# Linear attention and a gated feed-forward block: how the first batch's q is cast and turned, and the order of its first steps

## The chip, the cores and the metric

The kernel runs on one core of a Trainium2 chip. A core has a matrix engine (TensorE; PE in the profile, and PEld for its weight loads), a vector engine (VectorE, DVE), a scalar engine (ScalarE, ACT), GpSimd (POOL) and a sync engine (SP). Each engine works through its own instructions in order, and they wait for each other by semaphores. Here POOL and SP only issue DMAs, apart from a few small steps. The metric is the device time of one execution in microseconds. The kernel before takes 314.32 us in the median of five runs (313.93 to 314.49).

## The reference

Eight batches of eight heads, 576 tokens, 64 columns, go through linear attention, and the result through a gated feed-forward block over all 4608 tokens:

```python
phi = lambda x: np.where(x > 0, x, np.exp(x) - 1.0) + 1.0
q_p, k_p = phi(q), phi(k)
kv  = np.einsum('bhsd,bhse->bhde', k_p, v)
z   = np.sum(k_p, axis=2)
num = np.einsum('bhsd,bhde->bhse', q_p, kv)
den = np.einsum('bhsd,bhd->bhs', q_p, z)[..., None] + 1e-06
x   = (num / den).transpose(0, 2, 1, 3).reshape(B * S, H * D)
g   = x @ w_gate                       # 512 -> 1536
out = (g / (1 + np.exp(-g)) * (x @ w_val)) @ w_out   # 1536 -> 512
```

phi(x) is max(x, 0) + min(exp(x), 1), and the kernel computes it in that form, or, where x + 1 is at hand, as min(max(x + 1, 1), exp(x)).

## The kernel before

Everything is computed in fp16 with fp32 sums. The tokens of a batch are cut into 64 groups of nine neighbours: a partition holds one group (64 partitions for each half of the heads, 128 together), and j = 0..8 is the token in the group. Heads come in two parts, lp = 0 and 1, of two heads each per half. The feed-forward block works on nine groups g of 512 tokens (8 values of j of 64 tokens each). For each, layer 1 (`l1`, L292, with `l1_post`) takes 12 blocks fb of 128 columns, a gate and a value product in each, four steps of contraction c; layer 2 (`l2_mm`, L299) brings the 1536 columns back to 512. While group g is in these layers, the attention of the next batches is done between the products by the other engines. The order of all work is written out by hand: the order of the lines is the order on each engine, and nothing reorders it.

Loads are issued by POOL, mostly fp32 in memory to fp16 on the core, in a fixed order (L335 to L353): k and v of batch 0, the first weights, and so on; eight semaphores are used in turn, so a load waits for the one eight places ahead of it. Only q of batch 0 comes as fp32 by two SP DMAs, into `q32`, heads 0 and 1 first.

The change touches the time before the first full layer 1 block, in which batch 0 is prepared (L456 to L516), and the last token group of batch 0's q later on (`exp_q8`, `phi_q8`, called in `period0`). In the order of the program:

- Casts (L460 to L463): q32 to fp16 in `qr[0]`, head by head, three on DVE, the one of head 1 on ACT.
- `q_one` puts 1.0 into two pairs of PSUM banks; `q_turn` adds the transpose of q to it, by products with the identity `id16`: one product for each of two heads and each of eight j, 64 output rows each. So q + 1 stands there, turned.
- `q_exp(lp, h)` (ACT, L450 through L120) takes exp(q + 1 - 1) from half h of a pair to `qT`; `q_phi(lp, h)` (DVE, L454) joins it with the pair to phi(q).
- `exp_k`, `mx_k`, `mn_k`, `add_k` make phi of k: ek = exp on ACT, kp = max(k, 0), ek = min(ek, 1), kp = kp + ek on DVE.
- `zt` (L411) sums phi(k) over tokens by products, from kp before and from ek after the min, so that the sum needs no add; `zr_copy` spreads it to `Zr`. `kv_corner` (L185) makes k.v, 36 products of 64x64 for one operand and part; for lp = 0 it uses the added kp, for lp = 1 the kp and the ek one after the other. `r_copy` copies it to `R`.
- `t_corners` (L254) multiplies turned q with `Zr` (the denominators) and with `R` (the numerators); `lnrd` takes 1/x as exp(-ln x), four ACT steps for one lp; `x_t` (L424) multiplies the two into `xT`.
- `l1_mm` (L276) are the first two blocks of layer 1, taken step by step of c as chunks of `xT` get ready: c = 0 and 1 need `x_t(0,0)`, c = 2 and 3 the two halves of `x_t(0,1)`.
- `warm(n)` are n products without use of 128x512 (L124). `WARM` holds the six counts, in the order of the calls.

Of the kernel before, what the change touches and what calls it, by code (L numbers as in the profile page):

```python
# [9 lines left out]
AF = mybir.ActivationFunctionType  # L10
ALU = mybir.AluOpType
AX = mybir.AxisListType

P = 128
# [3 lines left out]
def kernel(  # L18
# [10 lines left out]
    nc = tc.nc  # L29

    B, H, S, D = q.shape
# [4 lines left out]
    J = S // C  # L36
# [3 lines left out]
    EPS = 1e-6  # L40
    SC = 4096.0
    NB = 3
    WARM = (4, 1, 4, 4, 2, 2)

    sb = ctx.enter_context(tc.tile_pool(name="sb", bufs=1))
    pp = ctx.enter_context(tc.tile_pool(name="ps", bufs=1, space=bass.MemoryType.PSUM))
# [2 lines left out]
    def many(shape, dt, name, n=2):  # L49
        return [sb.tile(shape, dt, name=f"{name}_{i}") for i in range(n)]  # L50

    kr = many([P, HL, J * D], FP16, "kr", NB)
    qr = many([P, HL, J * D], FP16, "qr", NB)
    vr = many([P, HL, J * D], FP16, "vr", NB)
    ek = many([P, 2, J, 2 * D], FP16, "ek")
    eq = many([P, HL, J * D], FP16, "eq")
    kp = many([P, 2, J, 2 * D], FP16, "kp")
    qp = many([P, 2, J, 2 * D], FP16, "qp")
# [6 lines left out]
    q32 = sb.tile([P, HL, J * D], FP32, name="q32")  # L65
# [16 lines left out]
    id16 = sb.tile([P, P], FP16, name="id16")  # L82
# [36 lines left out]
    def act(out, in_, func=AF.Copy, scale=1.0, bias=0.0):  # L119
        nc.scalar.activation(out=out, in_=in_, func=func, bias=bias, scale=scale)  # L120

    def warm(n, w=512, ps=None):
        for _ in range(n):
            nc.tensor.matmul(out=(ps or pp4[1][1])[:, 512 - w:512], lhsT=ones[:, :],  # L124
                             rhs=ones[:, 0:1].to_broadcast([P, w]), start=True, stop=True)
# [4 lines left out]
    def jl(t, b, lp):  # L130
        return t[b % 2][:, lp, :, :].rearrange("p j (l d) -> p l j d", d=D)

    def lj(t, b, lp):
        return t[b % NB][:, hs(lp), :].rearrange("p l (j d) -> p l j d", d=D)

    def exp_k(b, lp):
        act(jl(ek, b, lp), lj(kr, b, lp), AF.Exp)
# [4 lines left out]
    def mx_k(b, lp):  # L142
        nc.vector.tensor_scalar(out=jl(kp, b, lp), in0=lj(kr, b, lp), scalar1=0.0, scalar2=None, op0=ALU.max)  # L143

    def mn_k(b, lp):
        a = ek[b % 2][:, lp, :, :]
        nc.vector.tensor_scalar(out=a, in0=a, scalar1=1.0, scalar2=None, op0=ALU.min)  # L147
# [9 lines left out]
    def add_k(b, lp):  # L157
        a = kp[b % 2][:, lp, :, :]
        nc.vector.tensor_tensor(out=a, in0=ek[b % 2][:, lp, :, :], in1=a, op=ALU.add)  # L159
# [19 lines left out]
    def kv_corner(b, lp, t, first, last):  # L179
        ps = kvp[b]  # L180
        for j in range(J):
            for l2 in range(2):
                for hh in range(2):
                    rows = slice(C * hh, C * hh + C)
                    nc.tensor.matmul(out=ps[hh][D * l2:D * l2 + D, D * lp:D * lp + D],  # L185
                                     lhsT=t[b % 2][rows, lp, j, D * l2:D * l2 + D],
                                     rhs=vr[b % NB][rows, 2 * lp + l2, D * j:D * j + D],
                                     start=(first and j == 0), stop=(last and j == J - 1))
# [6 lines left out]
    def r_copy(b, l0, l1, engs):  # L195
        for hh in range(2):
            src = kvp[b][hh][:, D * l0:D * l1].rearrange("p (l d) -> p l d", d=D)
            if engs[hh] == "A":
                act(R[b % 3][:, l0:l1, hh, :], src)
            else:  # L200
                nc.vector.tensor_copy(out=R[b % 3][:, l0:l1, hh, :], in_=src)
# [38 lines left out]
    def units(g):  # L240
        us = [(u // J, u % J) for u in range(U * g, U * g + U)]
        res = []
        for b in sorted(set(u[0] for u in us)):
            js = [j for (bb, j) in us if bb == b]
            res.append((b, js[0], js[-1] + 1, C * us.index((b, js[0]))))
        return us, res
# [3 lines left out]
    def corners(ps, W, b, lp, j0, j1, c0):  # L250
        for l2 in range(2):
            rows = slice(D * l2, D * l2 + D)
            for hh in range(2):
                nc.tensor.matmul(out=ps[l2][C * hh:C * hh + C, c0:c0 + C * (j1 - j0)],  # L254
                                 lhsT=W[rows, lp, hh, :], rhs=qt(b, lp, hh, j0, j1)[rows],
                                 start=True, stop=True)
# [75 lines left out]
    for h in (0, 2):  # L332
        nc.sync.dma_start(out=q32[:, h:h + 2, :],
                          in_=q[0].rearrange("(l a) (c j) d -> (a c) l (j d)", a=2, j=J)[:, h:h + 2, :])
# [59 lines left out]
    def copy8(b, ps):  # L394
        nc.vector.tensor_copy(out=qT[b][:, :, 8, :, :].rearrange("p l h c -> p l (h c)"),
                              in_=ps[:, 256 * b:256 * b + P].bitcast(FP16).rearrange("p (l c) -> p l c", l=2))

    def exp_q8():
        act(eq[0][:, :, D * 8:D * 9], qr[0][:, :, D * 8:D * 9], AF.Exp)

    def phi_q8():
        r, e = qr[0][:, :, D * 8:D * 9], eq[0][:, :, D * 8:D * 9]
        nc.vector.tensor_scalar(out=r, in0=r, scalar1=0.0, scalar2=None, op0=ALU.max)
        nc.vector.tensor_scalar(out=e, in0=e, scalar1=1.0, scalar2=None, op0=ALU.min)
        nc.vector.tensor_tensor(out=qp[0][:, :, 8, :].rearrange("p a (l d) -> p a l d", d=D),
                                in0=e.rearrange("p (a l) d -> p a l d", l=2),
                                in1=r.rearrange("p (a l) d -> p a l d", l=2), op=ALU.add)

    def zt(b, lp, ps, t, first, last):
        for j in range(J):  # L410
            nc.tensor.matmul(out=ps[:, 0:2], lhsT=t[b % 2][:, lp, j, :], rhs=ob[:, 0:P:C],  # L411
                             start=(first and j == 0), stop=(last and j == J - 1))

    def zr_copy(b, lp, ps):
        nc.vector.tensor_scalar(out=Zr[b][:, lp, :, :], in0=ps[:, 0:2].unsqueeze(2).to_broadcast([P, 2, D]),
                                scalar1=1.0 / SC, scalar2=None, op0=ALU.mult)
# [9 lines left out]
    def x_t(g, lp, ps, l2s=(0, 1)):  # L426
        for l2 in l2s:
            xmul(xT[g % 2][:, 2 * lp + l2, :], ps[l2][:, :], rd[lp][:, l2, :])

    def t_corners(g, W, lp, ps):  # L430
        for (b, j0, j1, c0) in units(g)[1]:
            corners(ps, W[b], b, lp, j0, j1, c0)

    def q_one(pair_):
        for h in range(2):
            nc.tensor.matmul(out=pair_[h][:, :], lhsT=part[:, :], rhs=ones[:, 0:1].to_broadcast([P, 512]),
                             start=True, stop=False)

    def q_turn(lp, pair_):
        for l2 in range(2):  # L440
            for j in range(J - 1):
                nc.tensor.matmul(out=pair_[j // 4][D * l2:D * l2 + D, P * (j % 4):P * (j % 4) + P],  # L442
                                 lhsT=qr[0][:, 2 * lp + l2, D * j:D * j + D], rhs=id16[:, :],
                                 start=False, stop=(j % 4 == 3))

    def q_half(lp, h):
        return qT[0][:, lp, 4 * h:4 * h + 4, :, :].rearrange("p j h c -> p (j h c)")

    def q_exp(lp, h, pair_):
        act(q_half(lp, h), pair_[h][:, :], AF.Exp, bias=m1[:, 0:1])  # L450

    def q_phi(lp, h, pair_):
        a = q_half(lp, h)
        nc.vector.scalar_tensor_tensor(out=a, in0=pair_[h][:, :], scalar=1.0, in1=a, op0=ALU.max, op1=ALU.min)  # L454
# [2 lines left out]
    X = [pp4[0][0], pp4[3][0]]  # L457
    Y = [pp4[3][1], pp4[0][1]]
    qa, qb = pp4[2], pp4[0]
    nc.vector.tensor_copy(out=qr[0][:, 0, :], in_=q32[:, 0, :])  # L460
    act(qr[0][:, 1, :], q32[:, 1, :])
    nc.vector.tensor_copy(out=qr[0][:, 2, :], in_=q32[:, 2, :])
    nc.vector.tensor_copy(out=qr[0][:, 3, :], in_=q32[:, 3, :])  # L463
    warm(WARM[0])
    q_one(qa)
    q_one(qb)
    q_turn(0, qa)
    q_exp(0, 0, qa)
    q_exp(0, 1, qa)
    warm(WARM[1])  # L470
    q_turn(1, qb)
    q_exp(1, 0, qb)
    exp_k(0, 0)
    q_exp(1, 1, qb)
    warm(WARM[2])
    exp_k(0, 1)
    q_phi(0, 0, qa)
    q_phi(0, 1, qa)
    mx_k(0, 0)
    q_phi(1, 0, qb)  # L480
    mn_k(0, 0)
    mx_k(0, 1)
    zt(0, 0, X[1], kp, True, False)
    warm(WARM[3])
    zt(0, 0, X[1], ek, False, True)
    zr_copy(0, 0, X[1])
    warm(WARM[4])
    t_corners(0, Zr, 0, pp4[2])
    lnrd(pp4[2], 0)
    add_k(0, 0)  # L490
    q_phi(1, 1, qb)
    zt(0, 1, Y[0], kp, True, False)
    kv_corner(0, 0, kp, True, True)
    r_copy(0, 0, 1, "VV")
    warm(WARM[5], ps=X[0])
    mn_k(0, 1)
    t_corners(0, R, 0, X)
    zt(0, 1, Y[0], ek, False, True)
    zr_copy(0, 1, Y[0])
    x_t(0, 0, X, (0,))  # L500
    kv_corner(0, 1, kp, True, False)
    t_corners(0, Zr, 1, Y)
    lnrd(Y, 1)
    x_t(0, 0, X, (1,))
    kv_corner(0, 1, ek, False, True)
    r_copy(0, 1, 2, "VV")
    l1_mm(0, 0, pp4[2], (0,))
    l1_mm(0, 1, X, (0,))
    t_corners(0, R, 1, pp4[1])
# [264 lines left out]
```

## Time and profile before

| what | us |
|---|---|
| median of five runs | 314.32 |
| the profiled execution | 314.49 |
| its span | 312.7 |
| TensorE busy | 306.1 (98%) |
| DVE busy | 204.8 (66%) |
| ACT busy | 152.7 (49%) |
| first product of the first full layer 1 block (L292) starts at | 19.04 |

The span is the time from the first to the last instruction; 1.8 us lie around it. Busy shares are of the whole span. What happens in the first 20 us is not seen in them, but in the chain of what was waited for, read in the order of time, and in the order of instructions on each engine.

### The profile page before, as it was taken

How to read it: one execution, taken by the hardware profiler on the slowest of the kernel's cores; microseconds unless marked ns; L12 is line 12 of the kernel's file. 1: busy time of each engine (PE TensorE's matmuls, PEld its weight loads, DVE VectorE, ACT ScalarE, POOL GpSimd, SP SyncE). 2: the span in 40 equal slices, each digit the busy share in tenths (PEclk: the TensorE clock that was granted, in tenths of full speed). 3: DMA queues.
4: the chain of work that ended last, by engine and by line, in shares of the span. 5: the costliest groups of instructions: out<-in, count | busy, mean ns of one | idle time of the engine just before them, and what ended most of it. 6: DMA issues, size and time to landing. Idle time of an engine off the chain costs nothing.

```text
span 312.7 us, 5593 instructions
## 1 busy us (share of the span) xinstructions
PE 306.1 (98%) x2221; PEld 142.8 (46%) x2221; DVE 204.8 (66%) x361; ACT 152.7 (49%) x231; POOL 48.8 (16%) x73
## 2 busy tenths in 40 slices
PE   8989999999999999999999999999999999999994
PEld 4534444444544454445444544454444444444442
DVE  4854868999699667977697859874981434143410
ACT  4955959539633845375535643475330333133311
POOL 8745434400000410032001400000000000000000
PEclk9999999999999999999999999999999999999999
DMA  8999999998512594229612990514032300140014
GB/s 216 197 197 199 206 207 235 235 207 124 116 32 39 82 190 129 40 43 183 176 29 49 142 222 2 75 43 93 0 70 60 82 1 3 41 94 2 0 34 101
DMA packets 41178, 32.80 MB, mean 105 GB/s; under 512 B 16448, under 2 KB 36160, under 8 KB 41152
## 3 DMA queue, kind: packets, MB, share of 16 engines
q0 software_dynamic: 20480, 18.29, 37.4%
q1 hardware_dynamic: 20592, 14.13, 19.3%
q8 instruction: 17, 0.28, 0.3%
q14 instruction: 9, 0.07, 0.1%
q10 hardware_dynamic: 80, 0.03, 0.0%
HBM read 37.75 MB, written 9.44 MB: 151 GB/s over the span
## 4 chain that ended last, share of the span: by engine, by line
PE 96%; DMA 1%; DVE 1%; issue 0%; ACT 0%
PE pp L292 57%; PE pp L299 30%; PE pp L276 2%; PE pp L254 2%; PE pp L185 2%; DMA q<-in_q_dram 1%; PE pp L124 1%; DVE qT L454 0%; PE pp L411 0%; PE pp L442 0%; ACT qT L120 0%; PE pp L212 0%; PE pp L374 0%; DVE osb L322 0%; DVE kp L143 0%
## 5 line engine op out<-in xcount | busy, mean ns | idle before, releaser
L120 ACT ACTIVATE sil<-pp 128x512 f16<-128x512 f32 x108 | 63.4, 597 | 102.0 <-PE pp L292 101.0
L292 PE MATMUL pp<-xT,wg 128*128 128x512 f16 x416 | 106.8, 379 | 0.0
L292 PE MATMUL pp<-xT,wv 128*128 128x512 f16 x416 | 106.8, 379 | 0.0
L285 DVE SCALAR_TENSOR_TENSOR hT<-pp,sil 128x512 f16<-128x512 f32 x108 | 72.3, 681 | 49.3 <-PE pp L292 35.8
L299 PE MATMUL pp<-wo,hT 128*128 128x512 f16 (+2 forms) x444 | 97.1, 373 | 0.6 <-DVE osb L322 0.6
L299 PEld LDWEIGHTS <-hT 128*128 128x128 f16 x444 | 41.9, 98 | 49.9 <-issue 2.1
L292 PEld LDWEIGHTS <-wv 128*128 128x128 f16 x416 | 40.7, 98 | 49.1
L292 PEld LDWEIGHTS <-wg 128*128 128x128 f16 x416 | 40.7, 98 | 48.4
L322 DVE TENSOR_SCALAR osb<-pp 128x512 f32<-128x512 f32 (+1 forms) x19 | 12.9, 682 | 31.1 <-PE pp L299 31.1
L120 ACT ACTIVATE osb<-pp 128x512 f32<-128x512 f32 (+1 forms) x18 | 10.3, 574 | 34.8 <-PE pp L299 34.8
L120 ACT ACTIVATE ek<-kr 128x1152 f16<-128x1152 f16 x16 | 17.9, 1157 | 0.1
L120 ACT ACT_TABLE_LOAD x13 | 16.7, 1283 | 2.5 <-PE pp L292 2.4
L705 POOL COPY gate<-qT 128x1 f16<-128x1 f16 x4 | 1.3, 315 | 96.4 <-DMA qT<-qp 96.4
L229 DVE TENSOR_TENSOR qp<-qp,rden 128x1152 f16<-128x1152 f16 x12 | 16.2, 1347 | 0.0
L220 DVE TENSOR_REDUCE den<-prod 128x18 f32<-128x1152 f16 x12 | 16.1, 1343 | 0.0
L120 ACT ACTIVATE eq<-qr 128x1152 f16<-128x1152 f16 (+1 forms) x15 | 15.9, 1104 | 0.0
L271 DVE TENSOR_SCALAR xT<-pp 128x512 f16<-128x512 f32 (+1 forms) x14 | 8.8, 667 | 6.6 <-PE pp L254 6.6
L103 POOL DMA_DIRECT2D vr<-in_v_dram x16 | 11.8, 740 | 8.3 <-DMA kr<-in_k_dram 3.5
L103 POOL DMA_DIRECT2D kr<-in_k_dram x16 | 11.5, 722 | 9.3 <-DMA vr<-in_v_dram 3.0
L159 DVE TENSOR_TENSOR kp<-ek,kp 128x1152 f16<-128x1152 f16 x15 | 11.4, 758 | 0.5
L103 POOL DMA_DIRECT2D qr<-in_q_dram x14 | 10.1, 725 | 4.9 <-DMA qr<-in_q_dram 1.1
L147 DVE TENSOR_SCALAR ek<-ek 128x1152 f16<-128x1152 f16 x16 | 7.8, 486 | 4.5 <-ACT ek L120 4.5
(85 smaller groups left out, 180.9 us busy)
## 6 DMA issues: line engine op xcount, KB each, us to landing
out_dram<-osb SPq DMA_DIRECT2D x70, 128.0 KB, 2.8
kr<-in_k_dram POOLq DMA_DIRECT2D x16, 288.0 KB, 8.6
vr<-in_v_dram POOLq DMA_DIRECT2D x16, 288.0 KB, 9.4
qr<-in_q_dram POOLq DMA_DIRECT2D x14, 288.0 KB, 11.4
wg<-in_moe_w_gate_dram POOLq DMA_DIRECT2D x5, 256.0 KB, 9.7
wv<-in_moe_w_val_dram POOLq DMA_DIRECT2D x5, 256.0 KB, 10.1
q<-in_q_dram SPq DMA_DIRECT2D x2, 576.0 KB, 4.2
wo<-in_moe_w_out_dram POOLq DMA_DIRECT2D x2, 512.0 KB, 12.5
```

Of the source, the lines that this page charges most:

```text
L103: nc.gpsimd.dma_start(out=dst[b % NB][:, 2 * lp:2 * lp + 2, :], in_=src[b].rearrange("(l a) (c j) d -> (a c) l (j d)", a=2, j=J)[:, 2 * lp ...
L120: nc.scalar.activation(out=out, in_=in_, func=func, bias=bias, scale=scale)
L147: nc.vector.tensor_scalar(out=a, in0=a, scalar1=1.0, scalar2=None, op0=ALU.min)
L159: nc.vector.tensor_tensor(out=a, in0=ek[b % 2][:, lp, :, :], in1=a, op=ALU.add)
L185: nc.tensor.matmul(out=ps[hh][D * l2:D * l2 + D, D * lp:D * lp + D], lhsT=t[b % 2][rows, lp, j, D * l2:D * l2 + D], rhs=vr[b % NB][rows, 2 ...
L220: nc.vector.tensor_reduce(out=den[:, c, :], in_=prod[:, :, :].rearrange("p j (l d) -> p (j l) d", d=D), axis=AX.X, op=ALU.add)
L229: nc.vector.tensor_tensor(out=qv, in0=qv, in1=rden[:, c, :].unsqueeze(2).to_broadcast([P, 2 * J, D]), op=ALU.mult)
L271: nc.vector.tensor_scalar(out=dst, in0=ps[l2][:, c0:], scalar1=1.0 / SC, scalar2=None, op0=ALU.mult)
L285: nc.vector.scalar_tensor_tensor(out=hT[g % 2][:, fb, :], in0=ps[1][:, :], scalar=SC, in1=s[:, :], op0=ALU.mult, op1=ALU.mult)
L292: nc.tensor.matmul(out=ps[h][:, :], lhsT=w[:, c, P * fb:P * fb + P], rhs=xT[g % 2][:, c, :], start=(c == 0), stop=(c == 3))
L299: nc.tensor.matmul(out=l2p[(g, t)][:, n0:n1], lhsT=hT[g % 2][:, fb, P * t:P * t + P], rhs=wo[:, fb, n0:n1], start=(fb == 0), stop=(fb == F ...
L322: nc.vector.tensor_scalar(out=o[:, n0:n1], in0=ps[:, n0:n1], scalar1=1.0 / SC, scalar2=None, op0=ALU.mult)
```

## The change

q of batch 0 is cast into `qp[0]` in place of `qr[0]`: for each j the two heads of a part stand beside each other, 128 columns, and only j = 0 to 7 are cast. `q_turn` then takes one product with 128 rows for each j in place of two with 64. The ninth token, which is not turned here, is taken from `q32` by `exp_q8` and `phi_q8`. In the order of steps: `q_exp(1,1)` comes ahead of `exp_k(0,0)`; `q_phi(1,0)` ahead of `mx_k(0,0)`, and `q_phi(1,1)` right behind it; `mn_k(0,1)` follows `add_k(0,0)`; the second half of `zt(0,1)` with its `zr_copy` comes ahead of the numerators of lp = 0; both terms of `kv_corner(0,1)` and its `r_copy` come ahead of `t_corners(0, Zr, 1)`. The counts of warm products are (4, 2, 5, 4, 2, 1) in place of (4, 1, 4, 4, 2, 2).

```diff
-    WARM = (4, 1, 4, 4, 2, 2)
+    WARM = (4, 2, 5, 4, 2, 1)
...
+    def q8(t):
+        return t[:, :, D * 8:D * 9].rearrange("p (a l) d -> p a l d", l=2)
     def exp_q8():
-        act(eq[0][:, :, D * 8:D * 9], qr[0][:, :, D * 8:D * 9], AF.Exp)
+        act(q8(eq[0]), q8(q32), AF.Exp)
     def phi_q8():
-        r, e = qr[0][:, :, D * 8:D * 9], eq[0][:, :, D * 8:D * 9]
-        nc.vector.tensor_scalar(out=r, in0=r, scalar1=0.0, scalar2=None, op0=ALU.max)
-        nc.vector.tensor_scalar(out=e, in0=e, scalar1=1.0, scalar2=None, op0=ALU.min)
...
+        r = qp[0][:, :, 8, :].rearrange("p a (l d) -> p a l d", d=D)
+        nc.vector.tensor_scalar(out=r, in0=q8(q32), scalar1=0.0, scalar2=None, op0=ALU.max)
+        nc.vector.tensor_scalar(out=q8(eq[0]), in0=q8(eq[0]), scalar1=1.0, scalar2=None, op0=ALU.min)
+        nc.vector.tensor_tensor(out=r, in0=q8(eq[0]), in1=r, op=ALU.add)
...
     def q_turn(lp, pair_):
-        for l2 in range(2):
-            for j in range(J - 1):
-                nc.tensor.matmul(out=pair_[j // 4][D * l2:D * l2 + D, P * (j % 4):P * (j % 4) + P],
-                                 lhsT=qr[0][:, 2 * lp + l2, D * j:D * j + D], rhs=id16[:, :],
-                                 start=False, stop=(j % 4 == 3))
+        for j in range(J - 1):
+            nc.tensor.matmul(out=pair_[j // 4][:, P * (j % 4):P * (j % 4) + P],
+                             lhsT=qp[0][:, lp, j, :], rhs=id16[:, :],
+                             start=False, stop=(j % 4 == 3))
...
-    nc.vector.tensor_copy(out=qr[0][:, 0, :], in_=q32[:, 0, :])
-    act(qr[0][:, 1, :], q32[:, 1, :])
...
+    def q_cast(h):
+        return dict(out=qp[0][:, h // 2, 0:8, D * (h % 2):D * (h % 2) + D],
+                    in_=q32[:, h, 0:8 * D].rearrange("p (j d) -> p j d", d=D))
+    nc.vector.tensor_copy(**q_cast(0))
+    act(**q_cast(1))
...
     q_exp(1, 0, qb)
+    q_exp(1, 1, qb)
     exp_k(0, 0)
-    q_exp(1, 1, qb)
     warm(WARM[2])
     exp_k(0, 1)
     q_phi(0, 0, qa)
     q_phi(0, 1, qa)
+    q_phi(1, 0, qb)
     mx_k(0, 0)
-    q_phi(1, 0, qb)
+    q_phi(1, 1, qb)
     mn_k(0, 0)
...
     add_k(0, 0)
-    q_phi(1, 1, qb)
+    mn_k(0, 1)
     zt(0, 1, Y[0], kp, True, False)
     kv_corner(0, 0, kp, True, True)
     r_copy(0, 0, 1, "VV")
+    zt(0, 1, Y[0], ek, False, True)
     warm(WARM[5], ps=X[0])
-    mn_k(0, 1)
+    zr_copy(0, 1, Y[0])
     t_corners(0, R, 0, X)
-    zt(0, 1, Y[0], ek, False, True)
-    zr_copy(0, 1, Y[0])
     x_t(0, 0, X, (0,))
     kv_corner(0, 1, kp, True, False)
+    kv_corner(0, 1, ek, False, True)
+    r_copy(0, 1, 2, "VV")
     t_corners(0, Zr, 1, Y)
     lnrd(Y, 1)
     x_t(0, 0, X, (1,))
-    kv_corner(0, 1, ek, False, True)
-    r_copy(0, 1, 2, "VV")
```

More of the change, by code (lines that the diff above doesn't have):

```diff
@@ L396, in copy8 @@
                               in_=ps[:, 256 * b:256 * b + P].bitcast(FP16).rearrange("p (l c) -> p l c", l=2))
+    def q8(t):
+        return t[:, :, D * 8:D * 9].rearrange("p (a l) d -> p a l d", l=2)
     def exp_q8():
-        act(eq[0][:, :, D * 8:D * 9], qr[0][:, :, D * 8:D * 9], AF.Exp)
+        act(q8(eq[0]), q8(q32), AF.Exp)
     def phi_q8():
-        r, e = qr[0][:, :, D * 8:D * 9], eq[0][:, :, D * 8:D * 9]
-        nc.vector.tensor_scalar(out=r, in0=r, scalar1=0.0, scalar2=None, op0=ALU.max)
-        nc.vector.tensor_scalar(out=e, in0=e, scalar1=1.0, scalar2=None, op0=ALU.min)
-        nc.vector.tensor_tensor(out=qp[0][:, :, 8, :].rearrange("p a (l d) -> p a l d", d=D),
-                                in0=e.rearrange("p (a l) d -> p a l d", l=2),
-                                in1=r.rearrange("p (a l) d -> p a l d", l=2), op=ALU.add)
+        r = qp[0][:, :, 8, :].rearrange("p a (l d) -> p a l d", d=D)
+        nc.vector.tensor_scalar(out=r, in0=q8(q32), scalar1=0.0, scalar2=None, op0=ALU.max)
+        nc.vector.tensor_scalar(out=q8(eq[0]), in0=q8(eq[0]), scalar1=1.0, scalar2=None, op0=ALU.min)
+        nc.vector.tensor_tensor(out=r, in0=q8(eq[0]), in1=r, op=ALU.add)
     def zt(b, lp, ps, t, first, last):
@@ L459 @@
     qa, qb = pp4[2], pp4[0]
-    nc.vector.tensor_copy(out=qr[0][:, 0, :], in_=q32[:, 0, :])
-    act(qr[0][:, 1, :], q32[:, 1, :])
-    nc.vector.tensor_copy(out=qr[0][:, 2, :], in_=q32[:, 2, :])
-    nc.vector.tensor_copy(out=qr[0][:, 3, :], in_=q32[:, 3, :])
+    def q_cast(h):
[3 more added lines that the diff above has]
+    act(**q_cast(1))
+    nc.vector.tensor_copy(**q_cast(2))
+    nc.vector.tensor_copy(**q_cast(3))
     warm(WARM[0])
```

## The prediction

> **What bounds the kernel now.** I read the page's engine row and its chain first, then the chain in order of time for the first 22 us, then the order of instructions on TensorE, VectorE (DVE) and ScalarE (ACT) there, and last the DMA queues in windows of one microsecond.
>
> The page: first the engine row, then the clock row (tenths of full speed per slice), the row of instruction loads, and the chain's shares.
>
> ```profile
> PE 306.1 (98%) x2221; PEld 142.8 (46%) x2221; DVE 204.8 (66%) x361; ACT 152.7 (49%) x231; POOL 48.8 (16%) x73
> ...
> PEclk9999999999999999999999999999999999999999
> ...
> q8 instruction: 17, 0.28, 0.3%
> ...
> PE 96%; DMA 1%; DVE 1%; issue 0%; ACT 0%
> ```
>
> TensorE is the bound, and from 19.04 us on (first product of L292) it has almost no gap: a microsecond won or lost in the prologue arrives whole at the end, if TensorE afterwards finds everything in place. The change works in the prologue, so its chain decides (start, length, what):
>
> ```profile
> 0.74 3.77 DMA q<-in_q_dram
> ...
> 6.18 0.70 ACT qT L120
> 6.88 0.02 issue
> 6.90 1.29 DVE qT L454 x2
> 8.19 0.48 DVE kp L143
> 8.67 0.05 issue
> 8.72 0.39 PE pp L411 x9
> ...
> 13.37 0.39 PE pp L254 x4
> 13.76 0.34 PE pp L185 x36
> ...
> 16.86 0.89 issue
> 17.75 1.45 PE pp L276 x6
> ```
>
> Two things are to be seen. Up to 8.72 the chain goes through the first half of q (the two q_phi of L454), then `mx_k(0,0)` (L143), then the first z. And at 16.86 TensorE stands for 0.89 us on "issue": no semaphore holds it, in the middle of `l1_mm` (third product of c = 2; its operands were there for the first two).
>
> I take that stop for a late load of TensorE's own instructions. The DMA view of 15 to 16 us has this row, none in the windows before it:
>
> ```profile
> q0 software_dynamic: 380, 0.19, 138.8%
> q8 instruction: 1, 0.02, 5.9%
> ```
>
> Evidence: 17 loads of 0.28 MB are 16 KB each; 4442 TensorE instructions (products and weight loads) over 17 are about 256 each. When the DMA is idle (88, 125, 237, 262, 289 us), load k starts just as instruction 256k - 104 begins. Number 152 begins at 10.98 us, but q0 is full and the packet starts only at 15.26; it takes 0.95 and TensorE goes on at 17.75, at instruction 450. So from the request to going on it is 6.4 to 6.8 us, and the block is missed 298 instructions after the request's mark.
>
> Here a rule is to be weighed. The Trainium skill ("Runtime: NRT & Kernel Launch", section "Instruction fetch mechanics") says that blocks of 256 instructions are fetched while the current one executes, and that crossing a boundary costs one tail bump, mostly hidden. By the rule the stop is nothing of this kind, stays where it is in the program, and the change has only the longer chain worked out below (+0.62). The row says 0.89 us, with the queue of 16 KB loads starting 1.6 us before it. I follow the row.
>
> **The change, part by part.**
>
> *Instruction count.* `q_turn` goes from 32 products to 16 (8 per call instead of 16): -16. The warm products go from 17 to 18: +1. Each has a weight load: 30 instructions fewer before the stop's place. The 450th instruction, now in c = 2, is then old number 480. c = 3 ends at old 460, so the new place is ten products into L292. With TensorE reaching L292 at 18.65 (below), that is 18.65 + 9 x 0.216 = 20.6. The request: the mark falls into `kv_corner(0,0)`, at about 11.9 to 12.2 (old 11.0 to 11.3 plus 0.9). Plus the measured 6.4 to 6.8: 18.3 to 19.0. The block is there 1.6 us or more before it is needed, and the stop costs nothing; its cover is the products of c = 1 to 3 and the first ten of L292. Later loads: number 3 is asked at 41.8 instead of 40.8 and missed at 48.7 instead of 47.5; about the same 6.9 us. Without the stop, before's c = 3 would have waited for its input alone: `x_t(0,1)` ends at 16.42 + 0.69 = 17.11, c = 3 at 17.17, not 18.18. **Stop gone: -1.01.**
>
> *First turn and casts.* ACT's cast of head 1 has 512 instead of 576 columns: by the slope between 128x1152 (1153 ns) and 128x576 (683 ns), 0.63 us, done at 5.16. Eight products, still at half clock (107 ns apart in the trace at 5.05 to 6.23), start at 5.22, the fourth ends at 5.86, so `q_exp(0,0)` starts at 5.92 (6.18 before). The 0.26 is worth nothing on its own: DVE must first cast heads 2 and 3, which the DMA releases at 5.97. Those casts write runs of 64 at a stride of 128. No fp32 cast does so in the trace; the nearest row is L384, which writes the same strided form at 452 ns for 128x1152, as fast as the contiguous L147 (460). So I take the present rate: 33 ns less each, head 3 done at 6.79 (6.85 before). Bounds: 0.43 us each, or 0.69 if the strided write halves the rate (+0.5 on the path).
>
> *Second turn.* Products from 6.84, 56 ns apart; the fourth ends at 7.25; `q_exp(1,0)` 7.31 to 8.00 (7.42 before).
>
> *Order on DVE and ACT.* `q_phi(1,0)` now stands ahead of `mx_k(0,0)`. It waits for `q_exp(1,0)`: starts at 8.03. `mx_k(0,0)` follows 0.60 later (start to start, as at 7.51 and 8.10 before): 8.63, ends at 9.19, and behind it waits the first z on TensorE: 9.24 instead of 8.72, **+0.52**. `exp_k(0,0)` is behind `q_exp(1,1)`: 8.5 to 9.66 (9.16 before); `mn_k(0,0)` 9.74 to 10.20. The four warm products after the first z end at 10.39, so `mn_k` is hidden by 0.14 us; without it the z.ek part would wait for it. z.ek 10.39 (9.84): +0.54; `zr_copy` 10.80, `t_corners(Zr,0)` 11.15 and `lnrd(0)` on ACT 11.59 (11.05). `exp_k(0,1)` ends at 10.72 (10.79), nobody waits.
>
> `q_phi(1,1)` left its place behind `add_k(0,0)`; `mn_k(0,1)` stands there now, ending at 12.12 (12.52 before): z.ek of lp = 1 runs right after `kv_corner(0,0)`, `zr_copy(0,1)` ends 0.35 earlier. This hangs on no end: the next reader waits longer for something else.
>
> *Both k.v terms ahead of `t_corners(Zr,1)`.* `t_corners(R,0)` starts at 12.76 (12.21, +0.55), then kv kp and kv ek, 0.43 each with the step between (12.90 to 13.35 before): 13.96 for `t_corners(Zr,1)`, against 13.35. One z.ek of 0.37 less ahead of it, one kv more: **+0.62 in all**. Behind it waits `lnrd(1)`, four ACT steps of 2.59 together (13.80 to 16.39), now 14.41 to 17.01. `r_copy(0,1)` is 0.3 to 0.4 earlier, but `t_corners(R,1)` stays behind c = 0 at about 15.3 to 15.4 (15.00), so that gain has no taker. `x_t(0,1)` second half: 17.04 to 17.73. c = 3 starts at 17.78, L292 at 18.65. What is late next would be weights: `fb` = 2 lands at 17.32 (gate) and 18.09 (value), needed 18.65 and 19.5; covered. Layer 2 parts land 1.2 us or more ahead.
>
> *Last token group (period 0).* `exp_q8` and `phi_q8` read q32: one max on 128x256 in fp32 instead of fp16, 0.23 to about 0.36 us (estimate from the cast's rate). DVE then idles 0.36 us for `exp_k(1,0)`; hidden. No DMA is added or moved; POOL's load into `qr[0]` at 50 us loses a wait that was long met, and SP has nothing new.
>
> **Sum.** +0.62 - 1.01 = -0.39 us. The profiled execution took 314.49 (span 312.7 and 1.8 around it): 314.1. It is the slowest of the five shown; against the median of 314.32 it is 313.93, and I predict **313.9**.
>
> **Rivals.**
> 1. *The new order costs only about 0.2.* The 0.52 rests on DVE durations in a crowded stretch: `mx_k(0,0)` took 556 ns, the same form later 450; q's second half may land sooner; kv's pair may take 0.34 each. Together up to 0.4 less: 313.5. Against it: the wait of `q_phi(1,0)` on the second turn is in the order itself.
> 2. *The stop does not go* (the load comes later, or it was no load and sits at this place in the program). Then +0.62 stays: 314.9. For it: how long q0 holds the packet back (4 us here) is one sample of a full queue; other loads under traffic waited 3 to 4 us, none the 6 needed.
> 3. *The clock falls back* (the slower side). TensorE would idle 0.8 us from the last of the five warm products (8.42) to the first z (9.24), then do little dense work. The skill's "TensorE: Matmul & The Clock Gate", section "Part 1: The HAM clock gate", gives a busy window of about 3.4 us and half clock after an idle one. If it decided against the window up to about 9.65, warm and corner products until 13.06 double: four warm (0.75), corners (0.3), kv (0.4): +1.5, 315.4. [...]against it, the 0.89 us stop left the clock at 1.00.
> 4. *The casts lose their double rate*: +0.5, 314.4.
>
> **How the numbers follow.** A measurement of this kernel tells about 0.2% (0.63 us) from no change: faster is under 313.69, slower over 314.95. Main case 0.55, with its own range 313.4 to 314.4, since the stop's size and the chain each are good to some 0.3; about 4 in 10 of it are faster (0.22), the rest the same (0.33). Rival 1: 0.19, all faster. Rival 2: 0.16, on the border, 0.11 slower and 0.05 same. Rival 3: 0.05, slower. Rival 4: 0.05, 0.04 same and 0.01 slower. Sums: faster 0.41, same 0.42, slower 0.17. The range is 313.3 (rival 1's side) to 315.0 (rival 2 held).
>
> **What would show it.** Right: no "issue" piece near 17 us; the first z at about 9.2, `mx_k(0,0)` after three q_phi; `t_corners(Zr,1)` near 14.0; L292 from 18.5 to 18.8; a 16 KB load at about 16. Wrong: an "issue" piece some ten products into L292 (rival 2), products of 512 columns 0.43 apart after 9 us (rival 3), casts of 0.6 or more (rival 4), first z before 9.0 (rival 1).

## The result, and the profile after

The changed kernel takes 313.54 us (median), the one before 314.14 us in the same comparison. The ratio is 0.9981, with a 95% interval of 0.9976 to 0.9987: it is 0.6 us faster (0.4 to 0.75), a small gain, but clear of no change. The profiled execution took 313.39 us with a span of 311.6 (before: 314.49 and 312.7). The two profiles lie 1.1 us apart and the medians only 0.6, since before's profiled execution was 0.35 us slower than its median and the changed kernel's 0.15 faster.

The page after, engine row, clock row and instruction loads:

```profile
PE 304.8 (98%) x2206; PEld 141.6 (45%) x2206; DVE 204.9 (66%) x361; ACT 152.6 (49%) x231; POOL 48.3 (16%) x73
...
PEclk9999999999999999999999999999999999999999
...
q8 instruction: 17, 0.28, 0.3%
```

15 products fewer, and little else moves on these rows. The chain in order of time (start, length, what), first 22 us:

```profile
6.71 1.19 DVE qT L454 x2
7.91 0.02 issue
7.93 0.69 DVE qT L454
8.62 0.38 DVE kp L143
9.00 0.05 issue
9.04 0.39 PE pp L412 x9
...
12.62 0.35 PE pp L254 x2
...
14.73 0.38 PE pp L276
15.11 0.34 PE pp L254 x4
15.45 2.79 PE pp L276 x12
18.23 3.88 PE pp L292 x18
```

Three q_phi now stand ahead of `mx_k` (L143), and the first z starts at 9.04 in place of 8.72. But where before had six products, 0.89 us of "issue" and six more, there are twelve in one piece of 2.79 us. L292 starts at 18.07 in place of 19.04. The 16 KB load of instructions is still there in the window of 15 to 16 us (it starts at 15.52, 15.26 before):

```profile
q8 instruction: 1, 0.02, 6.1%
```

So the load is as late as it was, but the 450th instruction, which stood in c = 2, now begins only at about 20 us, some ten products into L292. TensorE no longer misses it. The four ACT steps of each `lnrd`:

```profile
11.37 0.69 ACT L120 ACTIVATE lnt<-pp,epsb 128x512 f32<-128x512 f32 x1 [0.79 <-PE pp L254]
12.09 0.63 ACT L120 ACTIVATE rd<-lnt 128x512 f16<-128x512 f32 x1
12.62 0.67 ACT L120 ACTIVATE lnt<-pp,epsb 128x512 f32<-128x512 f32 x1
13.33 0.63 ACT L120 ACTIVATE rd<-lnt 128x512 f16<-128x512 f32 x1
13.86 0.67 ACT L120 ACTIVATE lnt<-pp,epsb 128x512 f32<-128x512 f32 x1
```

The first starts 0.33 later than before (11.04), the fifth, which is `lnrd(1)`, only 0.07 later (13.80): ACT has no idle time between them now, where it had 0.16 us before. Of what the first part of the new order costs, the second, with one warm product fewer in it, gives back 0.26 us here.

### The profile page after: what moved, and what is told of

Read it like the earlier page. It is cut to its first block, busy times and chain, and to the rows that moved or that the text cites. A ratio compares the mean times of both kernels' runs of the same rounds, so it can differ in the third digit from the quotient of the medians.

```text
span 311.6 us, 5565 instructions
## 1 busy us (share of the span) xinstructions
PE 304.8 (98%) x2206; PEld 141.6 (45%) x2206; DVE 204.9 (66%) x361; ACT 152.6 (49%) x231; POOL 48.3 (16%) x73
## 4 chain that ended last, share of the span: by engine, by line
PE 95%; DVE 2%; DMA 1%; SPq 0%; issue 0%; ACT 0%; DVEq 0%
PE pp L292 58%; PE pp L299 30%; PE pp L276 2%; PE pp L254 2%; PE pp L185 2%; DMA q<-in_q_dram 1%; DVE qT L454 1%; PE pp L124 1%; DVE xT L425 0%; PE pp L412 0%; PE pp L212 0%; PE pp L374 0%; DVE osb L322 0%; SPq L333 0%; DVE qp L467 0%
## 5 line engine op out<-in xcount | busy, mean ns | idle before, releaser
L292 PE MATMUL pp<-xT,wg 128*128 128x512 f16 x416 | 106.8, 379 | 0.0
L292 PE MATMUL pp<-xT,wv 128*128 128x512 f16 x416 | 106.8, 379 | 0.0
L292 PEld LDWEIGHTS <-wv 128*128 128x128 f16 x416 | 40.7, 98 | 49.1
L292 PEld LDWEIGHTS <-wg 128*128 128x128 f16 x416 | 40.7, 98 | 48.4
L120 ACT ACTIVATE eq<-qr 128x1152 f16<-128x1152 f16 x14 | 15.5, 1153 | 0.0
```

The source lines that it names most:

```text
L292: nc.tensor.matmul(out=ps[h][:, :], lhsT=w[:, c, P * fb:P * fb + P], rhs=xT[g % 2][:, c, :], start=(c == 0), stop=(c == 3))
```

## The experiments

The theory is that of the prediction: the change gains because TensorE has 30 instructions fewer ahead of layer 1, so that it no longer misses a late block of its own instructions at its 450th; the new order of steps costs part of that. The rival: the gain comes from the new order and the casts, and the stop sits at its place in the program, or at its time, for another reason.

All runs, each beside runs of the kernel before on the same chip. "Stop" is TensorE's time on "issue" and where it falls among TensorE's instructions (450 is the 224th product in every row that has a stop); "z" is the start of the first z, L292 that of the first full block. These three are from the one profiled execution of each kernel, which can lie 0.3 us or more from the median. In all 14 profiles the execution ends 295.3 to 295.7 us after L292 starts: what a kernel gains here, it gains ahead of L292.

| kernel | TensorE instructions ahead of L292, against before | z | stop | L292 | median (before beside it) | ratio, 95% interval |
|---|---|---|---|---|---|---|
| before (profile shown) | 0 | 8.72 | 0.89 at 450 | 19.04 | | |
| after (profile shown) | -30 | 9.04 | none | 18.07 | 313.54 (314.14) | 0.9981 (0.9976 to 0.9987) |
| turn alone | -32 | 8.35 | none | 17.72 | 313.42 (314.17) | 0.9983 (0.9975 to 0.9990) |
| order alone | 0 | 9.29 | 0.45 at 450 | 19.28 | 314.68 (314.17) | 1.0019 (1.0011 to 1.0026) |
| turn alone, 16 products more | 0 | 8.58 | 0.63 at 450 | 18.75 | 314.23 (314.15) | 1.0010 (0.9998 to 1.0021) |
| after, 15 more, at the start | 0 | 9.71 | 0.95 at 450 | 19.80 | 315.03 (314.17) | 1.0029 (1.0019 to 1.0039) |
| after, 15 more, ahead of z | 0 | 9.06 | 1.08 at 450 | 19.30 | 314.52 (314.27) | 1.0014 (1.0005 to 1.0023) |
| before, 15 more, at the start | +30 | 10.00 | 2.68 at 450 | 25.08 | 320.20 (314.17) | 1.0191 (1.0178 to 1.0204) |
| before, 15 more, ahead of z | +30 | 8.53 | 2.68 at 450 | 22.31 | 318.04 (314.27) | 1.0124 (1.0101 to 1.0148) |
| turn, new order up to z only | -32 | 9.03 | none | 18.34 | 313.82 (314.15) | 0.9992 (0.9985 to 0.9998) |
| turn, new order behind z only | -32 | 8.66 | none | 17.93 | 313.25 (314.15) | 0.9976 (0.9968 to 0.9984) |
| the same, one warm product less | -34 | 8.35 | none | 17.67 | 313.27 (314.20) | 0.9977 (0.9965 to 0.9988) |
| after, warm counts of before | -32 | 9.03 | none | 18.44 | 313.74 (314.15) | 0.9991 (0.9984 to 0.9997) |
| after again | -30 | 9.17 | none | 18.19 | 313.57 (314.20) | 0.9984 (0.9976 to 0.9992) |

### The turn alone, and the order alone

The turn alone is the changed kernel with the lines of order and `WARM` of before:

```diff
-    WARM = (4, 2, 5, 4, 2, 1)
+    WARM = (4, 1, 4, 4, 2, 2)
...
-    q_exp(1, 1, qb)
     exp_k(0, 0)
+    q_exp(1, 1, qb)
...
-    q_phi(1, 0, qb)
     mx_k(0, 0)
-    q_phi(1, 1, qb)
+    q_phi(1, 0, qb)
```

and so on down to `x_t(0, 0, X, (1,))`.

> The casts, the 128-column turn and the last token group of the changed kernel, with the order of steps and the warm counts of before. TensorE has 32 instructions fewer ahead of layer 1. If the stop was a late block of instructions, missed at TensorE's 450th instruction: no idle piece near 17 us, first z at about 8.3 to 8.5, L292 from 17.6 to 18.1, time 313.2 to 313.6. If the gain comes from the new order (k.v ahead of the second q.z) and the stop belongs to its place in the program: the stop stays in c = 2 at about 16.7 to 17.7, L292 at 18.7 to 19.0, time 313.8 to 314.1.

It took 0.75 us less than before, with no stop: the part of the change that removes instructions has all of the gain by itself. The second and third product of c = 2, on TensorE (start, length, engine, line):

```profile
16.18 0.38 PE L276 MATMUL pp<-xT,wv 128*128 128x512 f16 x1
16.39 0.38 PE L276 MATMUL pp<-xT,wg 128*128 128x512 f16 x1
```

The order alone is the kernel before with those lines in the new order, its own casts, turn and counts.

> The order of steps of the changed kernel with the casts, turn and warm counts of before; TensorE has as many instructions ahead of layer 1 as before. If the stop is a late block: it stays at the third product of c = 2, and since the mark of its request (instruction 152 to 194) comes some 0.4 us later, it ends later too, at about 18.0; L292 at 19.1 to 19.4, time 314.2 to 314.8. If the gain comes from the order: L292 at 18.1 to 18.4, time 313.4 to 313.7.

0.5 us slower than before. The stop is at the same place, and ends at 17.99:

```profile
17.17 0.38 PE L276 MATMUL pp<-xT,wv 128*128 128x512 f16 x1
17.99 0.38 PE L276 MATMUL pp<-xT,wg 128*128 128x512 f16 x1 [0.45 <-issue]
```

The rival's first half has fallen as far as the order goes: by itself it loses.

### The count put back

To separate the count from the rest of the turn, the turn alone gets 16 products more without more columns, where TensorE waits for DVE anyway:

```diff
-    warm(WARM[2])
+    warm(20, w=102)
```

> The kernel with the turn alone (casts, turn and last token group changed, order and warm counts of before), and in it the 4 warm products of 512 columns ahead of the first z replaced by 20 of 102: the same columns, about the same time, 16 products more, so that TensorE's count is that of before. If the count alone decides: the stop is back at the third product of c = 2 (about 16.4 to 17.6), L292 at 18.7 to 19.1, and the time is back at 314.0 to 314.4. If the turn gains by itself: L292 at 17.7 to 18.0, 313.3 to 313.6.

0.8 us slower than the turn alone, and not to be told from before. (Its times fall into two groups, eight of 313.7 to 314.3 and six of 315.0 to 315.5, all at a granted clock of 0.999 or 1.00; why is open, and both groups are slower than the turn alone's median.) The stop is back at the third product of c = 2:

```profile
16.44 0.38 PE L276 MATMUL pp<-xT,wv 128*128 128x512 f16 x1
17.45 0.39 PE L276 MATMUL pp<-xT,wg 128*128 128x512 f16 x1 [0.63 <-issue]
```

So it takes the lower count for the turn to gain: with the count undone, nothing is left that can be measured. What the shorter casts and turn are worth once the stop is gone is not told apart by this, since while the stop stands, much of what they win ahead of it can go into standing longer. (That z is 0.23 later than with the turn alone is not the count: `mx_k` waited for k, which landed at 8.04 in this profile.) The same in the changed kernel, first with `warm(19, w=32)` in place of `warm(WARM[0])` at the very start:

> The changed kernel with its first 4 warm products of 512 columns replaced by 19 of 32 columns: 30 TensorE instructions more, at a time when TensorE waits for q anyway. If the stop is a late block: it comes back at the third product of c = 2 (about 16.8) and ends between 17.5 and 18.0; L292 at 18.7 to 19.1, time 0.5 to 1.0 above the changed kernel, 314.1 to 314.6. If it is not: as the changed kernel, L292 at 18.0 to 18.3, time 313.4 to 313.7.

The stop is back as expected, but the time is higher than expected, since this edit did a second thing: with 608 warm columns in place of 2048 at the start, the clock rose late. The five warm products of 512 columns ahead of the first z stood about 427 ns apart here, 218 in the changed kernel:

```profile
6.80 1.05 PE L442 MATMUL pp<-id,qp 128*128 128x128 f16 x8
7.65 2.23 PE L124 MATMUL pp<-ones 128*128 128x512 f16 x5
```

So once more, with `warm(20, w=128)` in place of the five products ahead of the first z, when the clock is up:

> The changed kernel with its 5 warm products of 512 columns ahead of the first z replaced by 20 of 128: the same columns and time, 15 products more, and nothing changed before the clock has risen. If the stop is a late block missed at TensorE's 450th instruction: it is back at the third product of c = 2, 16.7 to between 17.7 and 18.1; L292 at 18.9 to 19.3, time 0.7 to 1.1 above the changed kernel, 314.3 to 314.7. If the earlier run with 15 more was slow for its late clock alone: no stop, L292 at 18.1, 313.4 to 313.7.

First z at 9.06, 0.02 from the changed kernel, and everything up to c = 2 alike; then the stop, and 0.85 us more (+0.25 against before, where the changed kernel has -0.60):

```profile
16.53 0.38 PE L276 MATMUL pp<-xT,wv 128*128 128x512 f16 x1
17.99 0.39 PE L276 MATMUL pp<-xT,wg 128*128 128x512 f16 x1 [1.08 <-issue]
```

### The count raised

In the kernel before, 15 products more move the 450th instruction out of layer 1 altogether. With `warm(19, w=32)` at the start:

> The kernel before with its first 4 warm products of 512 columns replaced by 19 of 32 columns: 30 TensorE instructions more. If the stop is a late block: it moves 15 products towards the start of the program, to the end of the second term of k.v or c = 0 (about 14.0), lasts until about 17.1 to 17.7, and c = 0, the numerators of lp = 1, x_t and c = 1 to 3 all come behind it; L292 at about 20.5 to 21.2, time 315.6 to 316.4. If it is not: as before, 314.0 to 314.4.

and with `warm(19, w=108)` ahead of the first z:

> The kernel before with its 4 warm products ahead of the first z replaced by 19 of 108: the same columns, 15 products more, nothing changed before the clock has risen. If the stop is a late block: TensorE stands from about 14.0 (end of the k.v terms) to 17.5 or so. If the clock stays up through that, L292 at about 20.8 and 315.8 to 316.4; if the standing lets it fall to half, as in the run with 19 small products, L292 at 24 to 25 and 319 to 320.5. If there is no such block: 314.0 to 314.4.

The second is the clean one:

```profile
13.51 0.50 PE L185 MATMUL pp<-vr,ek 64*64 64x64 f16 x35
16.70 0.19 PE L185 MATMUL pp<-vr,ek 64*64 64x64 f16 x1 [2.68 <-issue]
16.82 0.60 PE L276 MATMUL pp<-xT,wg 128*128 128x512 f16 x1
17.21 0.63 PE L276 MATMUL pp<-xT,wv 128*128 128x512 f16 x1
```

TensorE stands at another line, between the last two products of `kv_corner`, which read the same tiles: what they have in common with the third product of c = 2 is only their number. It stands three times as long, as the theory has it: TensorE gets to the 450th 2.8 us earlier than before (14.0 for 16.86), while the packet starts only 0.9 earlier (14.37 for 15.26). And then the products of 512 columns are 0.4 us apart. The windows of two microseconds show why (length, busy times by engine, then the granted clock, DMA share, GB/s):

```profile
14.00:16.00 2.00, 0.01 (x2) 0.00 (x0) 0.55 (x2) 1.94 (x4) 1.78 (x3) 1.00 1.45 198
16.00:18.00 2.00, 1.30 (x4) 0.42 (x4) 0.22 (x1) 1.59 (x2) 0.75 (x1) 0.72 1.45 196
18.00:20.00 2.00, 2.00 (x8) 0.42 (x7) 0.62 (x2) 0.00 (x0) 1.11 (x2) 0.50 1.45 196
20.00:22.00 2.00, 2.00 (x10) 0.94 (x9) 0.67 (x2) 0.14 (x1) 1.07 (x2) 0.93 1.44 199
```

After 2.7 us of standing the clock was at half, from 16.86 to 20.28. So both things that were expected came in part: five of the six executions had a granted clock of 0.988 to 0.993 and took 317.7 to 319.35 us, and one had 1.00 and took 316.43, as expected for a clock that stays up. In the run with 19 products of 32 columns, the clock rose late as well, the stop was as long, and the clock stayed at half from 17.43 to 24.26; all of it together cost 6 us, where 1.4 to 2.2 had been expected.

In the seven profiles with a stop, the 16 KB packet started 2.25 to 2.49 us before TensorE went on, and its place was the same instruction. That a block of instructions is missing there is as good as shown. In the changed kernel the packet starts at 15.52; with the same delay (an estimate) the block is there at about 18.0, 2 us before it is needed. In these seven the packet starts 4.1 to 4.6 us after the 152nd instruction, at which the prediction puts the request. Why it waits so long (q0 moves data all the while) was not tried.

### What the order is worth

With no stop in the way, the two parts of the order can be taken apart (all with before's warm counts; the differences are each to before in the same comparison):

| | before's order behind z | new order behind z |
|---|---|---|
| before's order up to z | -0.75 | -0.90 |
| new order up to z | -0.33 | -0.41 |

The lower left:

> The turn with the changed kernel's order up to the first z and before's order behind it; warm counts of before. If the first part of the order costs its 0.3 us of a later first z and nothing gives it back: first z at 9.0, L292 at 18.0 to 18.2, 0.3 above the turn alone, 313.6 to 313.9. If it costs nothing: L292 at 17.7, 313.4.

the lower right:

> The changed kernel with the warm counts of before: one product fewer. TensorE waits for other engines at each of these places, so both theories expect no difference to the changed kernel beyond 0.2: first z at 9.0, L292 at 18.0 to 18.2, 313.4 to 313.7.

and the upper right, in which the fourth q_phi is put behind the second `zr_copy`:

> The turn with the order of before up to the first z (k's exp ahead of q's last, mx_k ahead of the third q_phi), the order of the changed kernel behind it (both k.v terms ahead of the second q.z), and the fourth q_phi put behind the second zr_copy; warm counts of before. If the second part of the order gains because ACT no longer waits for the second q.z: the four ACT steps of lp = 1 start at 13.2 (13.5 with the turn alone), L292 at 17.4 to 17.6, time 313.0 to 313.4, 0.2 to 0.3 below the turn alone. If that part is worth nothing: L292 at 17.7, 313.4.

The part up to the first z (q's last exp ahead of k's, q_phi ahead of `mx_k`) costs 0.4 to 0.5 us, in both columns. The wait is seen at the first z of the lower left, against 8.35 with the turn alone:

```profile
9.03 0.39 PE L412 MATMUL pp<-ob,kp 128*128 128x2 f16 x9 [0.78 <-DVE kp L143]
```

The part behind it (both k.v terms ahead of the second q.z) gains 0.08 to 0.15, too little for these intervals; its start on ACT in the upper right was 13.71, not the expected 13.2, in part since the second turn started 0.3 later in that profile (q landed later, and one cast took 0.66 us). One expectation failed: the changed kernel with before's warm counts is 0.2 us slower than with its own (in each comparison against before; the intervals touch). TensorE does not wait for others at each of those places. With z.ek now ahead of the numerators, the second of the two warm products there is in the way:

```profile
12.42 0.59 PE L124 MATMUL pp<-ones 128*128 128x512 f16 x2
12.94 0.41 PE L254 MATMUL pp<-qT,R 64*64 64x512 f16 x4
```

With the changed kernel's one, the numerators start at 12.55. (Of these 0.39 us, 0.16 stood at the second half of the first z already, 10.32 for 10.16; the rest is one warm product.) From the first z to L292 it takes 9.41 us here, 9.37 with the turn alone, and 9.03 and 9.02 in the two profiles of the changed kernel: in these profiles the new order behind the first z wins 0.3 us back only together with the changed warm counts. So it looked worth while to take the second of the two warm products out of the best version too:

> The turn, with before's order up to the first z and the changed kernel's order behind it, and one of the two warm products ahead of the numerators of lp = 0 taken out (counts 4, 1, 4, 4, 2, 1). If that second warm product stands on TensorE's path, as the changed kernel with the old counts showed (numerators at 12.94 in place of 12.55): numerators of lp = 0 at 12.0 to 12.2, the ACT steps of lp = 1 at 13.2, L292 at 17.3 to 17.6, 312.9 to 313.2. If not: as with two, 313.2 to 313.4.

> The changed kernel itself beside the run above on the same chip, to compare the two: 313.4 to 313.7, 0.3 to 0.5 above the version with before's order up to the first z.

No gain: 313.27 and 313.25 are the same. The numerators did start at 12.11, but the second q.z then came at 12.94 and the ACT steps of lp = 1 at 13.38. Both versions beat the changed kernel by 0.3 us in the medians (313.27 against 313.57 side by side), though the intervals of the ratios overlap.

## Why the prediction was right, and where it was off

The direction came as forecast and the size nearly: -0.6 us in the medians where the sum said -0.39, and 313.54 for 313.9 (half of that difference is the median of before, 314.14 in this comparison for 314.32). The main case was right in kind: the stop goes, the order costs. But both terms of the sum were too large. The stop was worth about 0.8 in place of 1.01, the new order cost about 0.15 in place of 0.62; that the two errors took each other back in part, and left the sum within 0.2 us, is luck. Of its signs, the missing "issue" piece, `mx_k` behind three q_phi and the late load came, and the first z nearly (9.04 for 9.2); the second q.z (13.39 for 14.0) and L292 (18.07 for 18.5 to 18.8) did not. In size it was rival 1 that came, with its 313.5.

*The stop.* Right, and for the reason given: shown by its return at the same instruction number in three kernels, and by its move to another line in two. The sum had -1.01 from one profiled execution, which was slow by 0.35 against before's median; all of that lies ahead of L292, in the stop and what is around it. In the medians the count is worth 0.8 (turn alone against turn with 16 more).

*The rule weighed against it* (the Trainium skill, "Runtime: NRT & Kernel Launch", section "Instruction fetch mechanics"). "Mostly hidden" fits 16 of the 17 loads: from 22 us on, the chain of before has no "issue" piece over 0.04 us. The first was not hidden: TensorE stood 0.45 to 2.68 us at it. Read as the prediction weighed it, the rule would have left +0.62 and a slower kernel.

*The order: +0.62 forecast, mis-sized.* From the turn alone to the changed kernel (new order and new warm counts) the medians go from -0.75 to -0.60 against before, so it cost 0.15. In the profiles L292 goes from 17.72 to 18.07. Two terms failed:

- *"+0.52" at the first z* was +0.32. The mechanism was right (q_phi waits for the second turn, `mx_k` behind it). Half of the difference is that the third q_phi started at 7.93, not 8.03, with the second turn and its exp 0.1 earlier. The other half is `mx_k(0,0)`, 450 ns in place of the 556 taken from before. That one was chance: it took 444 to 460 ns in 12 of the 14 profiles, but 556 in before's and 564 in the second of the changed kernel, where z came at 9.17. Two rows of the DVE order:

```profile
8.54 0.45 DVE L143 TENSOR_SCALAR kp<-kr 128x1152 f16<-128x1152 f16 x1
8.90 0.68 DVE L454 SCALAR_TENSOR_TENSOR qT<-pp,qT 128x512 f16<-128x512 f32 x1
```

- *"kv kp and kv ek, 0.43 each"*, from which the second q.z was to be 0.6 later. The k.v products start 0.24 after the numerators and the two terms 0.30 apart:

```profile
12.55 0.41 PE L254 MATMUL pp<-qT,R 64*64 64x512 f16 x4
12.79 0.48 PE L185 MATMUL pp<-vr,kp 64*64 64x64 f16 x36
13.09 0.49 PE L185 MATMUL pp<-vr,ek 64*64 64x64 f16 x36
13.39 0.41 PE L254 MATMUL pp<-qT,Zr 64*64 64x512 f16 x4
```

The step read in before, from the k.v products at 12.90 to the second q.z at 13.35, was not all work. The last of the 36 products started at 13.18; then TensorE waited for `zr_copy(0,1)`, which ended at 13.30. First `zr_copy(0,1)` before, then in the changed kernel:

```profile
13.01 0.29 DVE L415 TENSOR_SCALAR Zr<-pp 128x128 f16<-128x128 f32 x1 [0.48 <-PE pp L411]
```

```profile
12.42 0.29 DVE L416 TENSOR_SCALAR Zr<-pp 128x128 f16<-128x128 f32 x1
```

In all six profiles with the old order behind the first z, the second q.z starts 0.05 us after `zr_copy` ends. The new order puts `zr_copy(0,1)` ahead of the numerators, so the wait is gone. The prediction had that copy earlier too, but said that this "hangs on no end", and so counted the wait as work, twice. With 0.30 the second q.z starts at 13.39, 0.04 later than before, and ACT, which had 0.16 us to wait, goes straight on. Rival 1 had this pair at 0.34.

*The casts.* Right: 0.43 and 0.46 us with the strided write; rival 4 is out. (Later casts in other profiles took up to 0.58, and one 0.66.) "The 0.26 is worth nothing on its own" holds for the changed kernel, where z waits for the second turn.

*The clock.* TensorE idled 0.56 us ahead of the first z, and products of 512 columns behind it stood 0.22 us apart; rival 3 did not come in the profiles of the changed kernel. (One of its 39 executions in two comparisons took 314.93 us at a granted clock of 0.992, which may have been it.) Stops of up to 1.08 us left the clock up; those of 2.68 us did not, but for one execution. They were shorter than the window of 3.4 us that the prediction weighs, while the stretches at half behind them (3.4 and 6.8 us) are one and two such windows long.

*The last token group.* The max in fp32 took 0.48 us, not 0.36; DVE waited 0.50 us for `exp_k` behind it, so it stayed hidden.

## What to carry to other kernels

Where an engine stands on "issue" between two instructions that wait for nothing, count its instructions: if the place is a fixed number and an instruction load stands in the DMA view shortly before, the number of instructions ahead of it is a cost, above all while bulk loads fill the queues. Here 15 or 16 small products more cost 0.8 to 3.8 us, though TensorE had time for them where they stood; merging 32 small products into 16 saved 0.75, and nothing with the count put back. Both show only as a stop elsewhere. Separate such an effect from a new order of steps by putting the count back, with the same columns in more products. And before the step between two groups of products is taken for their length, see what the second waited for.

## What the hardware showed that was not expected

A fixed place 450 instructions into TensorE's stream was missed in seven kernels of different order and timing; the stop was 0.45 to 1.08 us with that place in layer 1, and 2.68 us with 15 products more ahead of it. The clock rose late in both runs with 19 products of 32 columns (608 in all) in place of 4 of 512 at the start: at 9.63 us in place of 5.12 in the changed kernel, at 10.6 in place of 6.24 in the one before, while it rose between 3.86 and 6.62 in the twelve other profiles. Whether the size of the products or the sum of their columns decides was not tried. Standing for 2.68 us was followed by half the clock for 3.4 us in one run and 6.8 in another; in one of the six executions of the first, the clock stayed at 1.00.
